# Fourier layer two: tile pairs in a written order of all engines, its second stage as seven block products, and third-sweep combinations kept by Fourier layer one

## The chip, the cores and the metric

The kernel runs on one core of one Trainium2 chip. The metric is the device time of one execution in microseconds; the time before is the median of three runs. The core has a matrix engine (PE, with its weight loads shown apart as PEld), a vector engine (DVE), an activation engine (ACT), GpSimd (POOL), and SyncE (SP), whose only work here is to issue DMA transfers. All data is float32; the matrix work is done in a split form, in which each operand is a rounded high part and a remainder, and three products (high·high, high·low, low·high) stand for one.

## The reference

Four layers in a row act on x (2048 rows of 640), each as `x = x + layer(layernorm(x))`: a sliding, dilated attention (A), a Fourier layer (B), and both again. The change is about the Fourier layers only:

```python
def _B_ref(x, dft_seq_re, dft_seq_im, dft_hid_re, dft_hid_im):
    a = jnp.einsum("bsd,ed->bse", x, dft_hid_re)
    b = jnp.einsum("bsd,ed->bse", x, dft_hid_im)
    y = jnp.einsum("ts,bse->bte", dft_seq_re, a) - jnp.einsum("ts,bse->bte", dft_seq_im, b)
    return y
...
x = x + _A_ref(_layernorm(x, axis=-1), A_wqkv, A_wo)
x = x + _B_ref(_layernorm(x, axis=-1), B_dft_seq_re, B_dft_seq_im, B_dft_hid_re, B_dft_hid_im)
x = x + _A_ref(_layernorm(x, axis=-1), A_wqkv, A_wo)
x = x + _B_ref(_layernorm(x, axis=-1), B_dft_seq_re, B_dft_seq_im, B_dft_hid_re, B_dft_hid_im)
```

## The kernel before

**Tiles.** The output of a Fourier layer is made in eight tiles of 256 rows, numbered 0 to 7. Each has two stages. The first multiplies the sequence matrices (real and imaginary, side by side as 512 columns) with the normalised x, and leaves five chunks of 128 hidden columns, called z, in PSUM. The second multiplies z with the hidden matrices and gives y: `ymm` takes a block of 128 rows, and for each of 5 chunks, 2 halves of 320 output columns, 3 split passes, and real and imaginary part issues one matmul 320 wide, so 60 for a block and 120 for a tile. `yout` adds y to x (a DVE addition for each half) and stores it.

**Pairs.** Tiles 0 and 1 are made on their own in `run`. Tiles 2 to 7 are made in three pairs by `pair`, and within a pair the first stage of chunks 0 to 3 is done as seven products of blocks instead of eight (m1 to m7, after Strassen's scheme). A pair has three sweeps, each over 8 steps i. In the first, products m5, m4 and m7 take 18 matmuls of width 512 a step; in the second, m2, m1 and the fifth chunk take 21; in the third, m3, m6 and the fifth chunk take 15. For each step, raw blocks of the sequence matrices are loaded (`s_raw`, the tile names are `win` and `xa`, seven buffers in all), partly combined by DVE (`combine`, line 1363), and split by ACT (the high part, line 1327) and DVE (the remainder, line 1328) into one of six views, two in tiles s0 and s1 and four in cells of the tiles r1_2 and r1_3. Combined blocks of x, which are made once in `run` and kept in HBM (`xc`), come back through `x_slot`. Behind each sweep, DVE and ACT put the products together from PSUM (lines 1421 to 1480) while PE does `ymm` of another block. In the third sweep, the first `ymm` of the pair's first tile is spread over the steps.

**Order.** Only PE's order is written out in a pair. The order of DVE, ACT and SP is chosen when the program is built, by a list scheduler with a timeline of its own. Each engine then executes its list strictly in order. In the attention layers the order of all engines is written out, step by step.

**Layers.** The class `LayerB` serves both Fourier layers: b1 (layer index 1) and b2 (layer index 3). The last pair of b1 is executed within the start of the second attention layer, which hangs its own first loads and transposes into it. The last tile of b2 has its second stage behind everything else, by `ytile` and `y_final`.

Of the kernel before, what the change touches and what calls it, by code (L numbers as in the profile page):

```python
# [20 lines left out]
D = 640  # L21
# [5 lines left out]
P = 128  # L27
# [130 lines left out]
    1: ((0, 0), (2, 1), 1),  # L158
    6: ((0, 1), (0, 0), -1),
}  # L160
NST = 16
FA = 64
GW = (512, 512, 512, 384)
# [6 lines left out]
def tile_layers(ctx: ExitStack, tc: tile.TileContext, x, wqkv, wo, cs, cst, wre, wim, out):  # L170
# [48 lines left out]
    xcb = [{m: dr.tile([P, NP, 2, 256], F32, name=f"xc_{l}_{m}") for m in XC} for l in range(2)]  # L219
# [846 lines left out]
    class LayerB:  # L1066
        def __init__(self, li):
            self.li = li
            self.xin, self.xout = xs[li], xs[li + 1]
            self.xn = {}  # L1070
            self.z = {}
            self.zt = {}
            self.xl, self.raw, self.ct = {}, {}, {}
            self.xc = xcb[li // 2]
            self.whole = {}
            self.ahead = {}
            self.late = []
            self.nraw = self.nhl = self.nx = self.nc_ = 0

        def ln_load(self, c, j):  # L1080
# [193 lines left out]
        def y_final(self, t):  # L1274
# [3 lines left out]
            for e in range(2):  # L1278
                o = xr[:, e * 320 : (e + 1) * 320]
                nc.vector.tensor_tensor(o, self.ym[e][:, :320], o, op=ALU.add)  # L1280
                nc.sync.dma_start(self.xout[c][:, j, e * 320 : (e + 1) * 320], o)

        def x_whole(self, side, i):
# [58 lines left out]
        def pair(self, p, nstats, hooks=None):  # L1342
# [53 lines left out]
            def ahead_b(i):  # L1396
# [3 lines left out]
                p22 = split(b22)  # L1400
                return x2, x1, p11, p22, lambda: (split(combine(b22, b11, b22, ALU.add)), split(b21))

            def ahead_c(i):
                b12, b22, b11 = raw(t2, i), raw(t2, NP + i), raw(t1, i)
                x6 = self.x_slot(6, i, ring)
                c3 = split(combine(b22, b12, b22, ALU.subtract))
                return x6, c3, split(b12), lambda: split(combine(b11, b11, b12, ALU.add))

            with tc.manual_schedule(engines={nc.tensor.engine}):
                m5, m4, m7 = banks("m0", "m1"), banks("xt", "t0"), banks("t1", "pq")  # L1410
                for i in range(NP):
                    ends = i == 0, i == NP - 1
                    x5, x7, c5, c4, c7 = self.ahead.pop(("a", p)) if i == 0 and ("a", p) in self.ahead else ahead_a(i)
                    self.product(m5, x5, c5, *ends)
                    self.product(m4, self.x_plain(*k2(i), 256), c4, *ends)
                    self.product(m7, x7, c7, *ends)
                    self.tick()
                b0 = ahead_b(0) if AH[0] else None
                m5s, m4s, ds = store("stg", CFG["bufs"]["stg"]), store("s2"), store("s3")
# [12 lines left out]
                for i in range(NP):  # L1432
# [5 lines left out]
                    c1, p21 = rest()  # L1438
                    self.product(m1, x1, c1, *ends)
                    self.product(f1, self.x_plain(*k2(i), 512), p21, False, i == NP - 1)  # L1440
                    self.tick()
                if hooks is not None:
                    views = cells[0] + cells[1] + CFG["views"]
# [50 lines left out]
        def run(self, nstats):  # L1494
# [6 lines left out]
            with ExitStack() as st:  # L1501
# [3 lines left out]
                for s in range(NST):  # L1505
# [6 lines left out]
                    self.z_mm(s, None, 1)  # L1512
                    self.tick()
                    for h in range(2):
                        ks = [k for k in range(KD) if R["y"][h][k] == s]
# [12 lines left out]
                self.evac(1)  # L1528
            for p in range(NPAIR - (nstats is not None)):
                self.pair(p, nstats)  # L1530

# [72 lines left out]
```

## Time and profile before

| what | value |
|---|---|
| median of three runs | 1736.29 us (1735.03, 1736.29, 1740.18) |
| span of the profiled execution, first to last instruction | 1734.8 us |
| PE busy | 1715.3 us of it |
| DVE, ACT, POOL busy | 1355.3, 824.7, 616.4 us |
| mean rate of the DMA engines | 242 GB/s |
| mean granted PE clock | 1.000 |
| b1's three pairs | from 455.6 us on, until about 855 us |
| b2's three pairs and its last tile | from 1313.1 us to the end |

The profile lists the busy time of each engine, then, for each line and shape of instruction, the count, the mean duration and what the engine waited for. Its windows give the same for any stretch of the span. The profiled execution's own time isn't listed apart; the median of the runs is 1.5 us above its span.

### The profile page before, as it was taken

The page shows a single profiled execution, that of the slowest core. Times are in us where ns is not written, and L with a number is a line of the kernel's source. Part 1 is how long each engine was busy: PE and PEld are TensorE (multiplying, and loading weights), DVE is VectorE, ACT ScalarE, POOL GpSimd, SP SyncE. Part 2 cuts the span into 40 slices and gives each one's busy share as a digit, 9 for nine tenths or more (in the row PEclk, how much of TensorE's full clock was granted, in tenths as well). Part 3 has the DMA queues.
Part 4 walks back from the last instruction along what each step waited for, and adds up shares of the span by engine and source line. Part 5 has one row for each costly group of instructions (what it writes and reads, how often), then busy time and mean ns, then how long its engine had stood idle before and what let it go on. Part 6 is the DMA issues. An engine that isn't in the chain of part 4 may idle for free.

```text
span 1734.8 us, 26552 instructions
## 1 busy us (share of the span) xinstructions
PE 1715.3 (99%) x8825; PEld 1496.1 (86%) x8825; DVE 1355.3 (78%) x2118; ACT 824.7 (48%) x1815; POOL 616.4 (36%) x570
## 2 busy tenths in 40 slices
PE   9999999999999999999999999999999999999999
PEld 7888888878888888888888889888888888888888
DVE  5999999978768667668639998899787677686673
ACT  5655645655445444445534434555444443443441
POOL 3899999940000000000019997899200000000000
PEclk9999999999999999999999999999999999999999
DMA  7768678959787687687547856698597867767761
GB/s 248 259 226 260 215 241 307 335 192 355 258 268 239 221 258 227 218 268 227 186 156 259 281 165 223 214 338 282 195 345 258 264 204 259 256 209 244 261 203 54
DMA packets 266713, 419.91 MB, mean 242 GB/s; under 512 B 22192, under 2 KB 144560, under 8 KB 266320
## 3 DMA queue, kind: packets, MB, share of 16 engines
q1 hardware_dynamic: 252400, 408.55, 71.2%
q10 hardware_dynamic: 14176, 9.67, 1.8%
q8 instruction: 70, 1.15, 0.3%
q14 instruction: 67, 0.55, 0.1%
HBM read 332.99 MB, written 85.14 MB: 241 GB/s over the span
## 4 chain that ended last, share of the span: by engine, by line
PE 86%; DVE 5%; POOL 3%; DMA 2%; issue 2%; ACT 2%; SPq 0%; DVEq 0%; ACTq 0%; POOLq 0%
PE m L499 18%; PE aux L1233 16%; PE t L1334 11%; PE m L1334 11%; PE aux L662 6%; PE pq L1334 6%; PE xt L1334 5%; PE m L1166 4%; PE t L1166 4%; PE xt L1166 2%; DVE pr L579 2%; DVE pr L622 1%; POOL pr L637 1%; POOL pr L582 1%; POOL pr L638 1%
## 5 line engine op out<-in xcount | busy, mean ns | idle before, releaser
L499 PE MATMUL m<-r,s 128*128 128x512 f32 (+1 forms) x1890 | 421.8, 378 | 0.2 <-ACT sg L514 0.2
L499 PEld LDWEIGHTS m<-r,s 128*128 128x128 f32 x1890 | 344.5, 188 | 54.7 <-ACT sg L514 1.6
L1327 ACT CAST r<-win 128x512 fp32r<-128x512 f32 x242 | 147.4, 621 | 168.2 <-DVE win L1363 80.4
L1233 PE MATMUL aux<-r2a,zo 128*128 128x320 f32 x768 | 226.0, 309 | 0.0
L579 DVE TENSOR_TENSOR pr<-pq,win 128x1280 f32<-128x1280 f32 x128 | 189.8, 1483 | 37.2 <-PE aux L1233 20.3
L637 POOL TENSOR_TENSOR pr<-pr 128x640 f32<-128x640 f32 x126 | 207.7, 1648 | 27.1 <-DVE pr L622 25.9
L1233 PE MATMUL aux<-pr,zo 128*128 128x320 f32 x704 | 208.0, 309 | 0.0
L582 POOL TENSOR_TENSOR pr<-pr 128x640 f32<-128x640 f32 x123 | 176.6, 1436 | 87.6 <-DVE pr L579 87.6
L622 DVE TENSOR_TENSOR pr<-pq,win 128x1280 f32<-128x1280 f32 x128 | 190.3, 1488 | 2.6
L1328 DVE TENSOR_TENSOR r<-win,r 128x512 fp32r<-128x512 f32 x242 | 162.7, 687 | 37.8 <-ACT r L1327 36.5
L300 POOL TENSOR_TENSOR stats<-stats,mhalf 128x1 f32<-128x1 f32 (+1 forms) x26 | 18.9, 728 | 445.9 <-ACT stats L294 445.9
L1334 PE MATMUL m<-r,r 128*128 128x512 f32 x600 | 153.0, 389 | 0.5 <-DVE r L1328 0.5
L1233 PEld LDWEIGHTS aux<-r2a,zo 128*128 128x128 f32 x768 | 144.1, 188 | 2.2
L1233 PEld LDWEIGHTS aux<-pr,zo 128*128 128x128 f32 x704 | 132.2, 188 | 2.4
L1334 PEld LDWEIGHTS m<-r,r 128*128 128x128 f32 x600 | 112.4, 188 | 24.0 <-DVE r L1328 1.0
L1334 PE MATMUL t<-r,r 128*128 128x512 f32 x492 | 132.0, 390 | 0.0
L638 POOL TENSOR_TENSOR pr<-pr 128x320 f32<-128x320 f32 x126 | 113.0, 897 | 9.9
L592 DVE TENSOR_REDUCE lg<-pr 128x64 f32<-128x640 f32 (+1 forms) x128 | 107.2, 837 | 11.4 <-POOL pr L582 11.3
L1363 DVE TENSOR_TENSOR win<-win,win 128x512 f32<-128x512 f32 x109 | 74.9, 691 | 49.9 <-DMA win<-cs_in 48.4
L1334 PEld LDWEIGHTS t<-r,r 128*128 128x128 f32 x492 | 92.4, 188 | 19.8
L1166 PE MATMUL m<-s,r 128*128 128x512 f32 x348 | 106.8, 395 | 1.7 <-ACT r L1103 0.9
L1166 PE MATMUL t<-s,r 128*128 128x512 f32 x348 | 105.2, 390 | 0.0
(299 smaller groups left out, 3245.6 us busy)
## 6 DMA issues: line engine op xcount, KB each, us to landing
win<-cs_in SPq DMA_DIRECT2D x346, 256.0 KB
r<-xc SPq DMA_DIRECT2D x240, 256.0 KB
win<-kvb SPq DMA_DIRECT2D x96, 440.0 KB
xa<-cs_in SPq DMA_DIRECT2D x120, 256.0 KB
win<-kvb SPq DMA_DIRECT2D x64, 360.0 KB
xc<-sg SPq DMA_DIRECT2D x28, 512.0 KB
xr<-xs SPq DMA_DIRECT2D x40, 320.0 KB
kvb<-stg SPq DMA_DIRECT2D x33, 320.0 KB
```

The lines of the kernel that those rows point to most:

```text
L499: nc.tensor.matmul(mt[g][:, : GW[q]], st[:, a, k], wq[q][:, b, k], start=n == 0, stop=n == 14)
L579: nc.vector.tensor_tensor(pr, q, wview(u, jp, 0, [[1, FE]]), op=ALU.mult)
L582: nc.gpsimd.tensor_tensor(pv[:, :, 0:10], pv[:, :, 0:10], pv[:, :, 10:20], op=ALU.add)
L592: nc.vector.tensor_reduce(rows(lgs[u], jp), pv.rearrange("p (a h) d -> p a h d", h=HE), axis=AX.X, op=ALU.add,)
L622: nc.vector.tensor_tensor(pr.rearrange("p j w (h d) -> p (j w) h d", d=DH), rows(lgs[u], jp).unsqueeze(3).to_broadcast([P, 2 * W, HE, DH]) ...
L637: g.tensor_tensor(pr[:, :, 0:4], pr[:, :, 0:4], pr[:, :, 4:8], op=ALU.add)
L638: g.tensor_tensor(pr[:, :, 0:2], pr[:, :, 0:2], pr[:, :, 2:4], op=ALU.add)
L1166: self.last = nc.tensor.matmul(self.z[t][k], self.xn[c][:, a, j, k * P : (k + 1) * P], self.ct[s][:, b], start=s == 0 and i == 0, stop=s = ...
L1233: self.last = nc.tensor.matmul(self.ym[e][:, :320], zt[(k, a, ri)][:, j2 * P : (j2 + 1) * P], w[:, e * 320 : (e + 1) * 320], start=(k, a, ...
L1327: nc.scalar.copy(hi, raw)
L1328: nc.vector.tensor_tensor(lo, raw, hi.bitcast(F32), op=ALU.subtract)
L1334: nc.tensor.matmul(bank, w(a, kb), hl[b], start=start and (a, b) == (0, 0), stop=stop and (a, b) == (1, 0),)
```

## The change

The pairs of b2, and its last tile, get a function of their own, `pairs7`. Fourier layer one keeps the old `pair`, with two additions. There are five parts.

1. **Order.** In `pairs7` the order of PE, DVE, ACT and SP is the order in which the code is written. Loads of a step are issued two steps ahead (`load(n + 2)`, `loadx(n + 2)`), and splits wait in a list (`fifo`) from which `fill` takes as many as there are free views, up to six.
2. **Second stage.** Of a tile's five chunks, the first three (`KS`) go through seven products of blocks: z is cut into 128-row halves and real and imaginary parts, the hidden matrices into halves of 320 columns. For each product 3 chunks × 3 passes are 9 matmuls; chunks 3 and 4 stay plain, with 12 matmuls for each of the four output blocks. The eight entries of `STAGES` name the bank's chain, the product, the plain block and the output block that is added afterwards. A chain goes on adding to the same bank after DVE has read it: chain 3 has four entries, chains 0 and 2 one, chain 1 two. Chains 0, 1 and 2 take bank aux0, chain 3 bank aux1.
3. **New operands.** `v_make` in b1 forms four combinations of the hidden matrices for each of the three chunks, splits them and stores them (`wvb`); `v_get` brings them back in the first pair of `pairs7`. `v_evac` replaces `zt_put`: it splits z as before, and forms and splits four sums for each of the three chunks.
4. **Kept combinations.** In the third sweep of b1's pairs, both combined sequence blocks of each step are stored to HBM (`keep`, `ccb`), and `pairs7` loads them instead of raw blocks, so that its third sweep has no `combine`. That lets the combined x of product m3, which was read plain from columns 0 to 255, come through `x_slot` as well (`x_keep`), and frees these columns for the operands of part 3.
5. **m6 into m1.** The product m6 goes on adding to m1's bank in place of a bank of its own.

```diff
+KS = (0, 1, 2)
+STAGES = (
+    (3, ("a11", "r0"), None, (0, 0)),
+    (0, ("a12", "i0"), (0, 0), (0, 0)),
+    (3, ("s2", "t2"), None, (0, 1)),
+    (1, ("s1", "t1"), None, (1, 1)),
+    (1, ("s4", "i1"), (0, 1), (0, 1)),
+    (3, ("s3", "u"), None, (1, 0)),
+    (2, ("a22", "t4"), (1, 0), (1, 0)),
+    (3, None, (1, 1), (1, 1)),
+)
...
+        def v_evac(self, t, raws, f, last=False):
...
+            def sums(raw, hi, lo, dg, ks):
...
+                v.tensor_tensor(a22, a21, a22, op=ALU.add)
+                v.tensor_tensor(a21, a21, a11, op=ALU.subtract)
+                v.tensor_tensor(a11, a11, a22, op=ALU.subtract)
+                v.tensor_tensor(a12, a12, a11, op=ALU.add)
...
+        def v_stage(self, t, n, tags=("aux0",) * 3 + ("aux1",)):
+            chain, prod, plain, (j, e) = STAGES[n]
...
+            if prod:
+                for k in KS:
+                    for a, b in PASSES:
+                        mms.append((self.zv[t][(prod[0], k)][a], self.wv[(prod[1], k)][b]))
...
+            h = self.half[(j, e)]
+            nc.vector.tensor_tensor(h, bank[:, :320], h, op=ALU.add)
...
+            def fill(most=99):
+                while fifo and held[0] < len(views) and most:
+                    fifo.pop(0)()
+                    held[0] += 1
+                    most -= 1
...
+                    product(bk["m3"], x[0], h("c3"), *ends)
+                    used()
+                    fill()
+                    product(bk["f2"], self.x_plain(*k1(i), 512), h("p12"), False, i == NP - 1)
+                    used()
+                    fill()
+                    product(bk["m1"], x[1], h("c6"), False, i == NP - 1, True)
+                    used()
+                    if 3 <= i < 6:
+                        self.v_stage(t1, (1, 0, 6)[i - 3])
+                    if i < NP - 1:
+                        continue
...
+                    for k, st in enumerate((2, 3, 5, 4, 7)):
+                        self.v_stage(t1, st)
...
+            def keep(i, n, raw):
+                nc.sync.dma_start(ccb[:, p, i, n], raw.rearrange("p r t -> p (r t)"))
...
+                    if i % 2 == 0 and 8 * p + i // 2 < 4 * len(KS):
+                        self.v_make(8 * p + i // 2)
...
+            if self.seven:
+                with tc.manual_schedule(engines=ENGINES - {nc.gpsimd.engine}):
+                    self.pairs7()
+                return
...
-    b2.ytile(NT - 1, 0, None)
-    b2.y_final(NT - 1)
```

What stands in the lists of the engines shows it at three places. The first is PE's list at the end of the third sweep of b2's first pair, before the change; t1 and m0, m1 are first-stage banks, aux0 and aux1 the second stage's.

```order
L1334 MATMUL t1_1949_13661<-r1_2_1732_12039,r1_1_1697_11760 128x512 x3
L1334 MATMUL m0_1995_14072<-r1_2_1732_12039,r1_1_1697_11760 128x512 x3
L1334 MATMUL m1_1996_14073<-r1_2_1732_12039,r1_1_1697_11760 128x512 x3
L1233 MATMUL aux0_2013_14198<-r2a_1821_12670,ot_1992_14056 128x320
L1233 MATMUL aux1_2014_14199<-r2a_1821_12670,ot_1992_14056 128x320
L1233 MATMUL aux0_2033_14397<-r2a_1821_12670,zo0_1989_14053 128x320
L1233 MATMUL aux1_2034_14398<-r2a_1821_12670,zo0_1989_14053 128x320
```

After the last 512-wide products come the last part of one `ymm` and then a whole `ymm` of 60 matmuls in new tiles of the two banks (one row stands for each run of matmuls). The same place of PE's list after the change:

```order
L1574 MATMUL t1_1981_13835<-r1_2_1750_12162,r1_1_1715_11883 128x512 x3
L1574 MATMUL m0_1977_13831<-r1_2_1750_12162,r1_1_1715_11883 128x512 x3
L1574 MATMUL m1_1978_13832<-r1_2_1750_12162,r1_1_1715_11883 128x512 x3
L1452 MATMUL aux1_2048_14436<-r1_0_1608_11228,zo0_2020_14227 128x320 x2
L1452 MATMUL aux0_2064_14598<-r2a_1839_12793,zo0_2020_14227 128x320 x2
L1452 MATMUL aux1_2048_14436<-r1_0_1608_11228,zo0_2020_14227 128x320 x2
L1452 MATMUL aux0_2064_14598<-pr0_1841_12798,zo0_2020_14227 128x320 x2
```

Entries 2, 3, 5 and 4 of `STAGES` follow, 9, 9, 9 and 21 matmuls, in turn on aux1 and aux0: the third goes on in the bank (buffer 2048) that the first filled, the fourth in that of the second. The second place is DVE's list there, first before the change (xt, t0, m0, m1 are the banks of m3 and m6, xr the rows of y).

```order
L1328 TENSOR_TENSOR r1_2_1732_12039<-xa_2029_14345,r1_2_1732_12039 128x2x256
L1477 TENSOR_TENSOR stg_1985_13977<-xt_1993_14070,stg_1985_13977 128x512
L1478 TENSOR_TENSOR s3_1941_13581<-xt_1993_14070,stg_1939_13579 128x512
L1480 TENSOR_TENSOR stg_1985_13977<-m0_1995_14072,stg_1985_13977 128x512
L1480 TENSOR_TENSOR stg_1985_13977<-m1_1996_14073,stg_1985_13977 128x512
L1246 TENSOR_TENSOR xr_2031_14384<-aux0_2013_14198,xr_2031_14384 128x320
```

A split into r1_2 stands ahead of the six instructions that put the products together, of which four are shown. DVE's list at this place after the change:

```order
L1520 TENSOR_TENSOR s1_2062_14565<-win_2060_14547,s1_2062_14565 128x512
L1515 TENSOR_TENSOR win_2060_14547<-win_2060_14547,win_2058_14543 128x512
L1520 TENSOR_TENSOR r1_2_1750_12162<-win_2059_14545,r1_2_1750_12162 128x2x256
L1515 TENSOR_TENSOR stg_2014_14149<-xt_2029_14243,stg_2014_14149 128x512
L1515 TENSOR_TENSOR s3_1969_13743<-t0_2030_14244,stg_1967_13741 128x512
L1515 TENSOR_TENSOR stg_2014_14149<-m1_1978_13832,stg_2014_14149 128x512
L1456 TENSOR_TENSOR xr_2018_14225<-aux1_2048_14436,xr_2018_14225 128x320
L1456 TENSOR_TENSOR qs_2019_14226<-aux0_2064_14598,qs_2019_14226 128x320
```

Three instructions that prepare the next sweep (the split into view s1, a combine, the split into r1_2) now stand directly ahead of those six, of which three are shown, and the addition that reads aux1 behind these. The third place is SP's list in the third sweep of b1's first pair, after the change (`cs_in` raw blocks, `xc` combined x).

```order
L1776 DMA win_878_5827<-cs_in 128x512
L1766 DMA r1_1_544_3397<-xc_0_6_123 128x2x256
L1863 DMA ccb_131<-win_875_5796 128x512
L1776 DMA xa_879_5829<-cs_in 128x512
L1863 DMA ccb_131<-xa_876_5798 128x512
L1776 DMA win_880_5831<-cs_in 128x512
```

The stores to `ccb` are new, two for each step, and stand between the loads.

More of the change, by code (lines that the diff above doesn't have):

```diff
@@ L218, in tile_layers @@
     qb = [[dr.tile([P, 2, NJ, FE], F32, name=f"qb_{c}_{q}") for q in range(NQ)] for c in range(NC)]
-    xcb = [{m: dr.tile([P, NP, 2, 256], F32, name=f"xc_{l}_{m}") for m in XC} for l in range(2)]
+    xcb = [{m: dr.tile([P, NP, 2, 256], F32, name=f"xc_{l}_{m}") for m in list(XC) + [3] * l} for l in range(2)]
+    wvb = dr.tile([P, len(KS), 4, 2, 320], F32, name="wvb")
+    ccb = dr.tile([P, NPAIR, NP, 2, 512], F32, name="ccb")
     c0b = dr.tile([P, NST, 2, 512], F32, name="c0b")
@@ L1405, in ahead_c, with rest @@
                 x6 = self.x_slot(6, i, ring)
-                c3 = split(combine(b22, b12, b22, ALU.subtract))
-                return x6, c3, split(b12), lambda: split(combine(b11, b11, b12, ALU.add))
+                keep(i, 0, combine(b22, b12, b22, ALU.subtract))
+                c3 = split(b22)
+                def rest():
+                    keep(i, 1, combine(b11, b11, b12, ALU.add))
+                    return split(b11)
+                return x6, c3, split(b12), rest
             with tc.manual_schedule(engines={nc.tensor.engine}):
@@ L1440, in pair @@
                     self.product(f1, self.x_plain(*k2(i), 512), p21, False, i == NP - 1)
+                    if i % 2 == 0 and 8 * p + 4 + i // 2 < 4 * len(KS):
+                        self.v_make(8 * p + 4 + i // 2)
                     self.tick()
@@ L1512, in run @@
                     self.z_mm(s, None, 1)
+                    if self.seven and 4 <= s < 4 + NP:
+                        self.x_keep(s - 4)
                     self.tick()
```

374 lines of the change are left out of this document (added).

## The prediction

> **What bounds the kernel now.** I read the page first, then the windows of the pairs, then the timeline at two places.
>
> ```profile
> span 1734.8 us, 26552 instructions
> PE 1715.3 (99%) x8825; PEld 1496.1 (86%) x8825; DVE 1355.3 (78%) x2118; ACT 824.7 (48%) x1815; POOL 616.4 (36%) x570
> PE 86%; DVE 5%; POOL 3%; DMA 2%; issue 2%; ACT 2%; SPq 0%; DVEq 0%; ACTq 0%; POOLq 0%
> ```
>
> PE is busy for all but 19.5 us, and the chain that ended last runs 86% over it. The windows below show that nearly none of the idle time lies in the pairs (columns: window, length, busy time of PE, PEld, DVE, ACT and POOL, granted clock, DMA share, GB/s). The first four rows are the three sweeps of b2's first pair and the `ymm` block behind the third; the last four are the sweeps of b1's first pair and the block ahead of its third sweep.
>
> ```profile
> 1313.10:1345.74 32.64, 32.42 (x143) 26.16 (x142) 23.29 (x38) 13.43 (x24) 0.00 (x0) 1.00 0.84 271
> 1354.54:1392.64 38.10, 38.10 (x172) 31.68 (x172) 25.13 (x39) 17.53 (x30) 0.00 (x0) 1.00 0.76 243
> 1401.44:1437.44 36.00, 36.00 (x181) 31.21 (x181) 24.74 (x43) 12.69 (x22) 0.00 (x0) 1.00 0.64 209
> 1437.44:1446.24 8.80, 8.80 (x58) 8.54 (x57) 7.79 (x14) 4.54 (x9) 0.00 (x0) 1.00 0.65 213
> 455.60:488.24 32.64, 32.57 (x145) 26.66 (x144) 23.85 (x39) 15.87 (x30) 0.00 (x0) 1.00 0.87 274
> 497.04:535.14 38.10, 38.10 (x171) 31.61 (x171) 26.44 (x42) 20.51 (x37) 0.00 (x0) 1.00 0.81 258
> 535.14:543.94 8.80, 8.80 (x61) 8.72 (x60) 8.80 (x16) 4.04 (x8) 0.00 (x0) 1.00 0.66 212
> 543.94:579.94 36.00, 36.00 (x181) 31.20 (x181) 23.30 (x40) 14.66 (x27) 2.10 (x2) 1.00 0.60 195
> ```
>
> So in the pairs a matmul removed is time won, as long as nothing that PE waits for comes later; and the reserve of the others is not large: DVE is busy for 0.71 of b2's first sweep, DMA for 0.84. Dividing rate by share, a full DMA moves about 325 GB/s (195/0.60; 271/0.84 is 323).
>
> What does a matmul cost when they follow each other?
>
> ```profile
> 1679.78 0.84 PE L1334 MATMUL t<-r,r 128*128 128x512 f32 x3
> ...
> 1681.14 1.52 PE L1334 MATMUL m<-s,r 128*128 128x512 f32 x6
> 1682.50 0.30 PE L1233 MATMUL aux<-r2a,zo 128*128 128x320 f32 x1
> ...
> 1684.11 0.31 PE L1233 MATMUL aux<-pr,zo 128*128 128x320 f32 x1
> 1684.26 0.85 PE L1334 MATMUL xt<-r,r 128*128 128x512 f32 x3
> ```
>
> Twelve of width 512 take 1682.50 - 1679.78 = 2.72 us, 0.227 each; twelve of width 320 take 1684.26 - 1682.50 = 1.76 us, 0.147 each. The durations (0.31) overlap and are not the price.
>
> **What the change removes.** For each of b2's tiles 2 to 7 the second stage falls from 120 matmuls of width 320 to 7 × 9 + 4 × 12 = 111. PE's list agrees: 1920 such matmuls in both Fourier layers before, 1200 + 666 now, 54 fewer. The first stage keeps its number (18 + 21 + 15 for a step). So 54 × 0.147 = **7.9 us** less on the path. The Trainium skill, page "TensorE: Matmul & The Clock Gate", section "Back-to-back issue gap", gives N/2.4 + 2.5 ns for an isolated matmul, 135.8 ns at 320 columns; by that the saving would be an estimated 7.3 us. The same section's sustained 131 ns at 512 columns isn't what this trace has (227 ns), so the row decides.
>
> **What it adds on DVE and ACT.** The third sweep loses two combines a step, 48 in all. Each tile gains the sums and their splits. For durations and spacing on DVE, I use the end of the third sweep in the first pair of b2:
>
> ```profile
> 1428.49 0.69 DVE L1328 TENSOR_TENSOR r<-xa,r 128x512 fp32r<-128x512 f32 x1
> 1434.12 0.69 DVE L1477 TENSOR_TENSOR stg<-xt,stg 128x512 f32<-128x512 f32 x1 [4.94 <-PE xt L1334]
> 1434.73 0.68 DVE L1478 TENSOR_TENSOR s<-xt,stg 128x512 f32<-128x512 f32 x1
> ...
> 1436.52 1.28 DVE L1480 TENSOR_TENSOR stg<-m,stg 128x512 f32<-128x512 f32 x2
> 1437.72 0.49 DVE L1246 TENSOR_TENSOR xr<-aux,xr 128x320 f32<-128x320 f32 x1
> L1212 DVE TENSOR_TENSOR zo<-s,zo 128x256 fp32r<-128x256 f32 x15 | 6.0, 419 | 1.1 <-PE aux L1233 0.6 <-ACT zo L1207 0.5
> 1435.97 0.62 ACT L1327 CAST r<-win 128x512 fp32r<-128x512 f32 x1
> ```
>
> A DVE instruction over 512 lasts 0.69 us and they follow each other at 0.61; 256 last 0.42; an addition of 320 lasts 0.49; a split by ACT 0.62. From 256 and 512, at 0.27 for each further 256, 1024 would last some 1.2 and 128 some 0.28. `v_evac` then costs a tile about 8 us of DVE (one of 1024, four of 512, six of 256, five of 128), where five splits of 512 cost 3.5 before. A pair therefore gains 9 us there and 4 in eight more additions, and loses 16 × 0.69 = 11: even. The sums of tile t2 fall into the next first sweep, whose DVE work is 8 × 5 × 0.61 = 24.4 plus 8, within 32.6 of products and 3.1 of entry 1. I cost this at nothing; what hides it is the two steps of splits that lie ready.
>
> **The waits it adds.** Before, a whole `ymm` of 60 matmuls, 8.8 us, stood behind each sweep in banks of its own; whatever DVE did meanwhile cost nothing. Now entries 2, 3, 5, 4, 7 stand there, and entry 5 adds to the bank that entry 2's addition must first have read. Between them PE has 18 matmuls, 2.64 us. On DVE, that addition is queued behind all that the list puts ahead of it. Take T as the end of the third sweep's last product (nine matmuls, 2.04 us, after m3's last). The view s1 is free at T - 1.9 (with 0.16 for the matmul's own tail). Then ACT's copy to -1.2; DVE's split, combine and split start at -1.16, -0.55 and +0.06; the six that put the products together at 0.66 and every 0.60 on until 3.67; the addition runs from 4.27 to 4.76. Before, the six could start at m3's end, as the idle 4.94 us ahead of the first shows. PE reaches entry 5 at T + 2.64 and stands until about 4.85: **2.2 us**, in pairs one and two, so 4.4. The third pair has no next sweep to prepare; its six start at T - 1.85 and the addition ends at 2.0, in time. Bounds: 0, if DVE gets its splits earlier than I think, and 4 for each, if the raw blocks for that combine land late.
>
> Behind the second sweep of pairs two and three, the same link: the last split starts at T - 0.4, four instructions follow, the addition ends at T + 3.1, PE stands for some 0.5 us: 1.0 in all (0 to 2). Behind the first sweep, only entries 0 and 6 follow, in different banks, and the next products' banks are free at T + 2: nothing. The last tile runs its eight entries over four banks; entry 0 wants aux1, which the addition of the previous tile's entry 7 frees at T + 12.0, PE is there at 11.9: 0.2 (0 to 2). Behind the last addition, one store ends the program as before.
>
> **The DMAs it adds.** One transfer costs SP's queue 0.33 to 0.38 us to issue, five a step are 1.9 us of 3.4: no bound.
>
> ```profile
> L1317 SPq DMA_DIRECT2D win<-cs_in x312: 327/332/1278, 428.0 to 1686.6; - x156
> L1307 SPq DMA_DIRECT2D r<-xc x240: 370/383/1347, 396.8 to 1686.1; - x120
> ```
>
> Bytes are closer. In b1, `v_make` moves 1.97 MB for a chunk (two loads and four stores of 0.328), 60 GB/s over a first sweep: 274 + 60 = 334 of 325, so about 0.9 us too much, and as much again in the second pair's first sweep. `keep` adds 4.2 MB to each third sweep, 116 GB/s: 195 + 116 = 311, just under. I put **2 us** on b1 (0 to 13, below). In b2's first pair the third sweep has five transfers of 0.262 MB and two of 0.164 a step, 13.1 MB or 40 us at 325 GB/s, against 34.7 of sweep and 8.8 of entries: 1 us (0 to 3) where it runs late.
>
> **Sum.** The span lacks 1.5 us to the median of the runs, which I carry unchanged: 1736.3 - 7.9 + 4.4 + 1.0 + 0.2 + 2 + 1 = **1737.0**.
>
> **Rivals.**
>
> *The waits are hidden.* If the additions reach their banks in time, and DMA keeps up, some 1 us is lost: 1736.3 - 7.9 + 1 = 1729.4. For it: DVE is idle for a quarter of these sweeps. Against it: DVE's written order, in which the addition can't pass what stands ahead.
>
> *b1's third sweeps become bound by DMA; slower.* In steps 0 to 2 there is no `ymm` between, so a step lasts 15 × 0.227 = 3.4 us; four loads and now two stores of 0.262 MB take 1.57/325 = 4.84 us. That is 1.44 × 3 steps × 3 pairs = 13 us in place of my 2: 1748. It decides if the loads lead by less than one step when the sweep begins: a store must leave a raw buffer before it can be loaded again, and there are seven. Half of it gives 1742.5. Against it: a whole `ymm` block ahead of the sweep, in which the DMA share was 0.66.
>
> *PE's clock.* A stop of PE of 2 us or more could cost clock afterwards. If the clock halves for as long as PE stood, 15 matmuls cost 0.147 more in each pair, 4.4 us with both: 1741.4. The row against it is the start of the kernel, where PE is busy for 3.69 us of 5 and the clock stays at 1.00:
>
> ```profile
> 0.00:5.00 5.00, 3.69 (x12) 1.45 (x13) 1.66 (x8) 1.73 (x4) 1.34 (x11) 1.00 0.64 196
> ```
>
> The Trainium skill's page "TensorE: Matmul & The Clock Gate", section "What's actually happening", has the clock halved after an idle window of about 3.4 us; by that rule stops of 2.2 us would cost nothing, stops of twice that might.
>
> *The new operands are slow.* t2, t4 and u lie in pieces of 80 columns. If such a matmul cost as much as one of 512, 27 × 6 × 0.08 = 13 us would be added: 1750. Against it: operands in pieces of 256 (r views) and whole ones (s views) take the same 389 ns today.
>
> ```profile
> L1334 PE MATMUL m<-r,r x600: 388/389/499, 455.6 to 1697.8; 128*128 128x512 f32 x150
> L1334 PE MATMUL m<-s,r x264: 389/389/398, 509.7 to 1703.0; 128*128 128x512 f32 x132
> ```
>
> **Chances.** A measurement of this kernel can tell about 0.3%, 5.2 us, from no change: 1731.1 to 1741.5. Forecast 0.58 (its own range 1732 to 1742), hidden waits 0.21, DMA in b1 0.12, clock 0.06, slow operands 0.03. Faster is the hidden waits, 0.21; slower is DMA and operands, half of the clock's case, which ends at the edge, and none of the forecast, 0.18; same is the rest, 0.61. The range takes half of the case of hidden waits below and half of the slower ones above: 1730 to 1745.
>
> **What would show it.** The saving: 666 matmuls of line 1452 at 0.147 apart. The waits: PE idle before line 1452, released by DVE's additions (line 1456), 2 us at a time, twice behind a third sweep. b1: PE idle in the windows of its pairs, with the DMA share at 0.9 and more. I am wrong if PE's idle time before line 1452 is below 2 us in all, or if idle time appears in the first stage's products of `pairs7` (line 1574), waiting for DVE or ACT, which I put at 1 us.

## The result and the profile after

The changed kernel is **slower**: 1750.57 us (median of four runs, 1748.35 to 1751.07) against 1736.0 of the kernel before (four runs, 1735.03 to 1740.18), a ratio of 1.0075 with a 95% interval of 1.0061 to 1.0089. The forecast was 1737.0 and the range ended at 1745. The profiled execution took 1748.35 us, its span 1746.6.

The page of the profile after, the lines that answer to those of before:

```profile
span 1746.6 us, 26782 instructions
PE 1712.0 (98%) x8771; PEld 1489.9 (85%) x8771; DVE 1370.6 (78%) x2166; ACT 834.9 (48%) x1838; POOL 614.7 (35%) x570
PE 72%; DMA 10%; DVE 10%; issue 3%; ACT 3%; POOL 2%; SPq 1%; ACTq 0%; DVEq 0%; POOLq 0%
```

54 matmuls fewer, as the change says. But PE's idle time rose from 19.5 to 34.6 us, and the chain that ended last, which ran 86% over PE, now runs 72% over it, with 10% each over DMA and DVE. The windows say in which stage. The columns are those of before; the first four rows are the first, second and third sweep of b2's first pair and the entries behind the third; the last three are b1's first pair: second sweep, the `ymm` block ahead of the third sweep, third sweep.

```profile
1315.95:1349.57 33.62, 32.95 (x146) 26.97 (x145) 26.49 (x42) 14.96 (x26) 0.00 (x0) 1.00 0.86 285
1358.37:1396.47 38.10, 38.10 (x170) 31.55 (x169) 26.30 (x39) 19.81 (x33) 0.00 (x0) 1.00 0.98 323
1405.27:1443.64 38.37, 35.32 (x173) 29.84 (x172) 21.59 (x40) 15.29 (x27) 0.00 (x0) 1.00 0.99 322
1443.64:1462.04 18.40, 11.48 (x62) 10.73 (x60) 11.27 (x19) 3.91 (x7) 0.00 (x0) 0.81 0.53 191
495.92:534.02 38.10, 37.80 (x168) 31.06 (x167) 27.78 (x49) 20.79 (x42) 0.00 (x0) 1.00 0.93 318
534.02:543.80 9.78, 9.78 (x66) 9.56 (x65) 9.78 (x18) 5.12 (x10) 0.00 (x0) 1.00 1.00 345
543.80:579.80 36.00, 36.00 (x182) 31.21 (x181) 25.03 (x44) 14.53 (x27) 1.74 (x2) 1.00 0.87 298
```

In b2's first pair the second and third sweep run with the DMA engines full (0.98 and 0.99). The third sweep stands for 3 of its 38.37 us. The entries behind it take 18.40 us, 6.9 of them idle, and PE's granted clock is 0.81 on their average. In b1 the DMA share is up from 0.81, 0.66 and 0.60 to 0.93, 1.00 and 0.87, and PE hardly stands. The list of PE's waits (what waited, for what; us in all, times, the longest) has these ahead of everything that both kernels share:

```profile
PE aux L1452 <- DVE xr L1456: 6.4, 4, 3.7
PE aux L1452 <- DMA r2a<-wvb: 3.2, 1, 3.2
PE xt L1574 <- DMA r<-xc: 3.1, 2, 1.6
```

And PE's timeline behind the third sweep, first in pair one, then in pair two (start, length, instruction, count, in brackets the idle time ahead of it and what ended it):

```profile
1449.20 1.00 PE L1452 MATMUL aux<-r2a,zo 128*128 128x320 f32 x3 [3.21 <-DMA r2a<-wvb]
1453.88 2.23 PE L1452 MATMUL aux<-r,zo 128*128 128x320 f32 x7 [3.67 <-DVE xr L1456]
...
1456.44 2.24 PE L1452 MATMUL aux<-pr,zo 128*128 128x320 f32 x9
1458.52 0.31 PE L1452 MATMUL aux<-r2a,sg 128*128 128x320 f32 x1
...
1589.39 1.29 PE L1452 MATMUL aux<-r,zo 128*128 128x320 f32 x7 [2.23 <-DVE xr L1456]
```

Pair two has the wait that I forecast, 2.23 us, and nothing else of note. Pair one has it at 3.67, behind a wait of 3.21 for t1 that I didn't forecast, and then matmuls that follow each other more slowly: the 18 from 1453.88 to 1458.52 take 4.64 us, where at 0.147 each they would take 2.65. From the start of b2's pairs to the end, the trace has 1746.6 - 1315.95 = 430.65 us against 1734.8 - 1313.11 = 421.69 before: 8.96 more, in spite of 7.9 saved, so some 17 us of new waits. 13.2 of them lie in pair one's third sweep and its entries (38.37 + 18.40, against 34.76 + 8.79 in experiment e6 below, where they run without a wait). The rest of the span's difference, 2.8 us, has arisen by the time b2's pairs begin.

The late t1 and r<-xc lead to SP. Its list around the second stage behind b2's second sweep (SPq: when each DMA was issued and how long the issue took), first before, then after:

```profile
1391.33 0.38 SPq L1307 DMA_DIRECT2D r<-xc  x1
1393.58 0.33 SPq L1317 DMA_DIRECT2D win<-cs_in  x1
1394.00 0.39 SPq L1307 DMA_DIRECT2D r<-xc  x1
1395.96 0.93 SPq L1317 DMA_DIRECT2D xa<-cs_in  x2
1400.76 0.93 SPq L1317 DMA_DIRECT2D win<-cs_in  x2
1405.99 0.34 SPq L1253 DMA_DIRECT2D y_out<-xr  x1
```

```profile
1392.90 0.87 SPq L1352 DMA_DIRECT2D r<-wvb  x2
1393.82 0.47 SPq L334 DMA_DIRECT2D xr<-xs  x1
1405.99 0.35 SPq L1268 DMA_DIRECT2D y_out<-xr  x1
1406.44 1.10 SPq L1494 DMA_DIRECT2D win<-ccb  x1
...
1444.28 0.81 SPq L1354 DMA_DIRECT2D r2a<-wvb  x2
```

In both, the store of y can't be issued before 1405.99, when DVE's addition behind `ymm` is done. Before, the list scheduler had put loads for the coming sweep ahead of it. Now the order of the code is SP's order, and the loads for the coming steps stand behind the store: SP issues nothing for 11.7 us, and from 1393.6 to 1406.0 the DMA engines have a share of only 0.29. The last row shows a second thing: t1's six loads stand last among the 24 loads of the second stage's operands, and the last two of them are issued at 1444.28, when the third sweep's products are over (1443.64). That gave a theory with three parts for pair one (the store in SP's list; the 24 loads of the second stage's operands inside sweeps that are full already; the splits ahead of the put-together operations on DVE), and a fourth, apart from them, for what the change adds ahead of b2's pairs. The rival: the pair's bytes are simply too many, wherever they are issued.

### The profile page after: what moved, and what is told of

The parts are those of the page before. It is cut to its first block, busy times and chain, and to the rows that moved or that the text cites. A ratio compares the mean times of both kernels' runs of the same rounds, so it can differ in the third digit from the quotient of the medians.

```text
span 1746.6 us, 26782 instructions
## 1 busy us (share of the span) xinstructions
PE 1712.0 (98%) x8771; PEld 1489.9 (85%) x8771; DVE 1370.6 (78%) x2166; ACT 834.9 (48%) x1838; POOL 614.7 (35%) x570
## 3 DMA queue, kind: packets, MB, share of 16 engines
q8 instruction: 70, 1.15, 0.3%
## 4 chain that ended last, share of the span: by engine, by line
PE 72%; DMA 10%; DVE 10%; issue 3%; ACT 3%; POOL 2%; SPq 1%; ACTq 0%; DVEq 0%; POOLq 0%
PE m L512 19%; PE aux L1248 7%; PE aux L675 6%; PE t L1574 5%; PE m L1574 5%; PE aux L1452 4%; PE m L1793 3%; DMA win<-cs_in 3%; PE t L1793 3%; PE m L1181 3%; PE pq L1574 3%; PE t L1181 3%; PE xt L1574 2%; PE xt L1793 2%; PE xt L1181 1%
## 5 line engine op out<-in xcount | busy, mean ns | idle before, releaser
L1248 PE MATMUL aux<-r2a,zo 128*128 128x320 f32 x480 | 141.4, 309 | 0.0
L1248 PE MATMUL aux<-pr,zo 128*128 128x320 f32 x440 | 130.1, 309 | 0.0
L526 ACT COPY stg<-m 128x480 f32<-128x480 f32 x96 | 53.5, 557 | 94.0 <-PE m L512 88.2
L1248 PEld LDWEIGHTS aux<-r2a,zo 128*128 128x128 f32 x480 | 90.1, 188 | 1.4
L1248 PEld LDWEIGHTS aux<-pr,zo 128*128 128x128 f32 x440 | 82.6, 188 | 1.6
L675 PE MATMUL aux<-r2a,ot 128*128 128x320 f32 x540 | 83.7, 310 | 0.0
L675 PEld LDWEIGHTS aux<-r2a,ot 128*128 128x128 f32 x540 | 80.4, 188 | 1.5 <-ACT wa L498 0.3
```

The source lines that it names most:

```text
L675: nc.tensor.matmul(m[:, :320], oT[(c, j)][:, a, k], wo_s["w"][:, b, k, e * 320 : (e + 1) * 320], start=(i, k) == (0, 0), stop=(i, k) == (2 ...
L1248: self.last = nc.tensor.matmul(self.ym[e][:, :320], zt[(k, a, ri)][:, j2 * P : (j2 + 1) * P], w[:, e * 320 : (e + 1) * 320], start=(k, a, ...
```

## The experiments

The twelve were timed in three groups, e1 to e4, e5 to e8 and e9 to e12, each on a chip of its own beside the kernel before. us is the median; the medians of before lie between 1735.9 and 1736.6. By the intervals, the difference of two runs is known to some 3 to 4 us.

| run | us | ratio to before, 95% interval |
|---|---|---|
| the change | 1750.6 | 1.0075, 1.0061 to 1.0089 |
| e1 loads between | 1758.2 | 1.0127, 1.0113 to 1.0142 |
| e2 no early splits | 1745.2 | 1.0047, 1.0031 to 1.0064 |
| e3 both | 1751.8 | 1.0087, 1.0073 to 1.0101 |
| e5 stores deferred | 1745.5 | 1.0046, 1.0033 to 1.0060 |
| e12 = e2 + e5 | 1738.6 | 1.0013, 1.0003 to 1.0024 |
| e6 = e12 + loads between | 1734.0 | 0.9982, 0.9970 to 0.9993 |
| e11 = e6, x stores later | 1736.3 | 0.9991, 0.9981 to 1.0002 |
| e10 = e6 without kept sums | 1761.4 | 1.0143, 1.0130 to 1.0157 |
| e4 b1's and run's part only | 1743.8 | 1.0041, 1.0028 to 1.0055 |
| e7 of it, keeping only | 1739.8 | 1.0016, 1.0006 to 1.0026 |
| e8 of it, making only | 1738.0 | 1.0005, 0.9996 to 1.0013 |
| e9 of it, x stores only | 1737.5 | 1.0008, 0.9999 to 1.0016 |

### e1: the loads between the sweeps, and e3: with e2

In `pairs7` the loads of t4, t2 and u leave the sweeps:

```diff
-                if p == 0 and sw > 0:
-                    for _ in range((0, 1, 2)[sw]):
-                        if gets:
-                            self.v_get(*gets.pop(0))
+                if p == 0 and sw == 2 and gets:
+                    self.v_get(*gets.pop(0))
...
                         self.yout(tp, 0, None)
+                        for _ in range(9):
+                            self.v_get(*gets.pop(0))
...
                         self.yout(tp, 1, None)
                         self.v_halves()
+                        for _ in range(9):
+                            self.v_get(*gets.pop(0))
```

> The 18 loads of t4, t2 and u are issued in the two stretches between the sweeps of b2's first pair (nine in each, while the second stage of tile 1 runs, DMA share 0.34 and 0.31 in after) and t1's six one a step from the third sweep's first step on; nothing else is changed. Theory A (these loads, in sweeps whose DMA share is 1.0 already, are what costs the first pair its 10 us: two waits for r<-xc, 1.57 and 1.48, one for t1, 3.21, a late chain on DVE, 3.67, and slow matmuls behind the stop, some 2.6): all goes but a wait of about 2.2 for DVE, so some 8 to 10 us less than after: 1741 to 1743, the PE idle time that r<-xc and r2a<-wvb release below 1 us in the first pair. Rival B (the bytes of the pair are too many wherever they are issued): the wait moves to the start of the next sweep, 0 to 3 us less than after: 1748 to 1751.

Measured: 1758.2, slower than the change by 7.6, against both theories. SP's list in e1, around the same place:

```profile
1399.57 1.25 SPq L1768 DMA_DIRECT2D r<-xc  x2
1400.87 0.46 SPq L334 DMA_DIRECT2D xr<-xs  x1
1414.53 0.35 SPq L1268 DMA_DIRECT2D y_out<-xr  x1
1414.93 1.66 SPq L1354 DMA_DIRECT2D r<-wvb  x3
...
1420.05 0.50 SPq L1354 DMA_DIRECT2D qs<-wvb  x1
1420.65 0.37 SPq L1494 DMA_DIRECT2D win<-ccb  x1
```

My edit had put the nine loads behind `yout`, so behind its store. They were issued from 1414.93 on, when the third sweep had already begun, and that sweep's own loads had to wait until they were out: PE stood 7.10 us for r<-xc there, and 3.81 us in the second sweep, ahead of which my edit had put the other nine. The run didn't test the bytes; what it shows is that a place in SP's list ahead of or behind a waiting store matters more than the stage in which the load stands.

> The two edits together. Theory A: the loads are worth 8 to 10 us and the splits another 2 to 4 (2.2 in each of pairs one and two): 1737 to 1740, equal to the kernel before within 0.3%; what is left against 1728.4 (before less 7.9) is some 5 us in b1 and in b2's run and some 3 of small waits. If both rivals held: 1748 or more.

Measured: 1751.8, for the same reason 12 us above what the theory had. Against e1 the late splits gain 6.5.

### e2: no splits ahead of the put-together operations

```diff
-                fill()
+                if sw < 2 or i < NP - 1:
+                    fill()
...
                     product(bk["m3"], x[0], h("c3"), *ends)
                     used()
-                    fill()
+                    if i < NP - 1:
+                        fill()
```

and the same behind the product with p12.

> In the last step of each third sweep of b2's pairs one and two no further splits for the next sweep are put ahead of the six operations that put the products together; they follow in the second stage's entries. Nothing else is changed. Theory A (PE stands before entry 5 since DVE's addition of entry 2 is queued behind splits and six put-together operations): pair two's 2.23 us before line 1452 go to below 0.5; of pair one's 3.67 some 2 go; total 1746 to 1748. Rival B (the splits that are put off are missing at the start of the next first sweep): the same 2 us appear before the first products of the next pair, 1750 or more. Rival C (DVE isn't the cause, the wait stays): 1750.

Measured: 1745.2, 5.4 less than the change, where theory A had 1746 to 1748. DVE's and PE's timelines in pair two:

```profile
1580.74 0.68 DVE L1520 TENSOR_TENSOR s<-win,s 128x512 fp32r<-128x512 f32 x1
1581.34 0.68 DVE L1515 TENSOR_TENSOR stg<-xt,stg 128x512 f32<-128x512 f32 x1
...
1583.73 1.28 DVE L1515 TENSOR_TENSOR stg<-m,stg 128x512 f32<-128x512 f32 x2
1585.34 0.49 DVE L1456 TENSOR_TENSOR xr<-aux,xr 128x320 f32<-128x320 f32 x1 [0.33 <-PE aux L1452]
```

```profile
1585.14 1.48 PE L1452 MATMUL aux<-r2a,zo 128*128 128x320 f32 x9
1586.46 1.19 PE L1452 MATMUL aux<-r,zo 128*128 128x320 f32 x7
```

The six operations start as soon as m3's bank is done, the addition of entry 2 now waits for PE (0.33) and not the reverse, and entry 5 follows entry 3 without a stop. The wait didn't come back at the next sweep. So the place of the splits in DVE's list was the cause, as the prediction had it.

### e5: the two stores of tile 1 two steps later

```diff
-                        self.yout(tp, 0, None)
+                        self.yout(tp, 0, None, 2)
...
-                        self.yout(tp, 1, None)
+                        self.yout(tp, 1, None, 2)
...
                 self.v_flush()
+                self.tick()
```

> After, with only the two stores of tile 1 in b2's first pair (y_out<-xr behind the first and the second sweep) issued two steps later, at the next sweep's second step. Theory A (SP issues in a written order now; each of these stores waits some 13 us for DVE's addition, and the loads of x, of the raw blocks and of the second stage's operands that stand behind it are late: in e1 SP stood from 1401.3 to 1414.5 and r<-xc came 7.1 us late): the two waits of after for r<-xc (1.57 and 1.48) go, and with an earlier queue part of the 3.21 for t1 and of DVE's lateness: 3 to 8 us less than after, 1743 to 1747. Rival B (the DMA engines are full in the third sweep, share 1.0, and set its pace whatever the queue's order): within 1.5 us of after, 1749 to 1751.

Measured: 1745.5, 5.1 less than the change. The waits for r<-xc are gone, and the one for t1 is down from 3.21 to 1.57, though the third sweep's DMA share is still 0.92. In the 12.5 us ahead of that sweep the share is 0.91, where the change has 0.35. Theory A holds; the DVE wait stays (3.72), which is e2's matter.

### e12 and e6: all of it, with the loads in the sweeps or between them

e12 is e2 and e5 together. e6 has e1's loads as well, but ahead of the second stage's load of x, which the store follows:

```diff
+                        for _ in range(9):
+                            self.v_get(*gets.pop(0))
                         self.ymm(tp, 0, 0, KD)
...
+                        for _ in range(9):
+                            self.v_get(*gets.pop(0))
                         self.ymm(tp, 1, 0, KD)
```

> After, with the stores deferred, the late splits of e2, and the 18 loads of t4, t2 and u issued ahead of the second stage's load of x in each of the two stretches (nine and nine, ahead of what waits there), t1's six one a step from the third sweep's first step on. Theory A: the first pair loses neither r<-xc nor t1 (below 1 us of PE idle time in the third sweep and its entries together), and what is left over the kernel before is b1's part, some 8 us by e4, against 7.9 saved: 1735 to 1738. Rival B (bytes): 1743 or more, r<-xc or r2a<-wvb still late by 3 us and more.

> e6 with the 24 loads of the second stage's operands where after has them (one and two a step in the second and third sweep), so only the stores' place in SP's list and the late splits are mended. e2 alone is worth 5.4 us and e5 alone 5.1. Theory A (the stores were the trouble in the queue; the loads then fit): 1734 to 1737, within 2 us of e6. Rival B (their bytes in sweeps with a DMA share of 1.0 cost by themselves): 1738 to 1742, r2a<-wvb late by 1.5 us or more, as in e5.

Measured: e12 1738.6, e6 1734.0 (one of its twelve executions took 7498 us, for which I have no reading; the median of the other eleven is 1733.4, and the differences below use that). In e12, whose profiled execution was its longest (1743.32), the wait for t1 is 2.84 us still; in e6 there is none. The windows of e6's third sweep of pair one and of its entries:

```profile
1405.93:1440.69 34.76, 34.76 (x173) 29.98 (x172) 25.70 (x46) 16.90 (x30) 0.00 (x0) 1.00 0.98 336
1440.69:1449.48 8.79, 8.79 (x62) 8.79 (x60) 4.95 (x10) 0.85 (x2) 0.00 (x0) 1.00 0.36 111
```

Both are PE's bare work. So the bytes of the whole pair fit, and the rival is out. With the loads where the change has them the time is 1738.6 - 1733.4 = 5.2 us longer. From the start of b2's pairs to the end e6 takes 1731.5 - 1316.62 = 414.9 us, 6.8 less than before, of 7.9 that the matmuls save; e12 takes 1741.4 - 1321.19 = 420.2. What in the loads costs these 5 us isn't told apart, since e6 moves the 18 loads out of the sweeps and also issues t1's six earlier. In e12 the last two of these six are issued at 1445.56, as late as in the change; in e6 the last one is issued some 12 us before the third sweep ends:

```profile
1428.49 0.42 SPq L1354 DMA_DIRECT2D r2a<-wvb  x1
```

A run with only t1's loads moved ahead would tell. The edits from the change to e6 gain 17.2 us: 5.4 and 5.1 by e2 and e5 alone, 5.2 by the loads, and the remainder, 1.5, isn't told apart. What keeps e6 from being 7.9 us faster than before is mainly what the change adds ahead of b2's pairs (e4 below).

### e10: without the kept combinations

b2's third sweep loads raw blocks and combines two of them a step, as before; b1 keeps nothing.

```diff
-                    raws[n] = [pre(p, i, 0), self.s_raw(t2, i, wide), pre(p, i, 1)]
+                    raws[n] = [self.s_raw(*a, wide) for a in ((t2, NP + i), (t2, i), (t1, i))]
...
+                def d0():
+                    b22, b12, b11 = raws[n]
+                    combine(b22, b12, b22, ALU.subtract)
+                    half(n, "c3", b22)
```

> e6 without the kept combinations: b1 stores none, and b2's third sweep loads three raw blocks a step and combines two of them on DVE, as the kernel before did. Theory A (the keeping stores cost 3.2 us in b1 and DVE has the time for the combines in b2, 77% busy): 1730 to 1732, 2 to 4 less than e6. Rival B (DVE is bound there: 16 more instructions of 0.61 us spacing in a sweep, 9.8 us, ahead of the same additions, so PE waits for them): 1738 to 1745, idle time before the first stage's products and before line 1452 in b2's third sweeps.

Measured: 1761.4, 28 us more than e6: rival B, and far beyond its price. DVE's timeline in the third sweep of pair one:

```profile
1418.86 0.69 DVE L1515 TENSOR_TENSOR win<-win,win 128x512 f32<-128x512 f32 x1
1420.37 0.69 DVE L1520 TENSOR_TENSOR s<-win,s 128x512 fp32r<-128x512 f32 x1 [0.82 <-ACT s L1519]
...
1422.69 0.68 DVE L1515 TENSOR_TENSOR win<-xa,win 128x512 f32<-128x512 f32 x1
1424.19 0.69 DVE L1520 TENSOR_TENSOR s<-win,s 128x512 fp32r<-128x512 f32 x1 [0.82 <-ACT s L1519]
```

In the written order a combined block goes DVE (combine), ACT (high part), DVE (remainder) with nothing between, so DVE stands 0.82 us for ACT each time: some 2.1 us for a combined block from the combine's start to the next instruction, not two times 0.61. Two such blocks are 4.2 us, and a step's products take PE 3.4. From the start of b2's pairs to the end e10 takes 447.0 us, 32 more than e6. PE's waits explain some 18 of it: 11.9 before line 1452, in stops of up to 3.1 us, and 6.8 before the third sweeps' products, against 0.5 and nothing in e6. The other 13.5 are busy time of PE, 423.9 us against 410.4 for the same 2084 matmuls, with the granted clock at 0.50 behind the four longest stops.

### e4, e7, e8, e9: what the change adds ahead of b2's pairs

e4 keeps b1's stores and the making of the operands and the eight stores of x, and gives b2 the pairs and the last tile of before, which read none of it. e7, e8 and e9 have one of the three each.

```diff
-            if self.seven:
-                with tc.manual_schedule(engines=ENGINES - {nc.gpsimd.engine}):
-                    self.pairs7()
-                return
```

> All that the change adds ahead of b2's pairs (the keeping stores of b1's third sweeps, the making of t4, t2, u and t1, the eight stores of x in b2's run) stays, and b2's pairs and last tile are as in the kernel before, which don't read what was kept. Theory A (these transfers cost b1's pairs 2.5 us and b2's run 2.4 us on PE, as after's trace has it against before's): 1736 + 4 to 6 = 1740 to 1742. Rival B (the difference of the two traces there is jitter from one execution to the next): 1736 to 1737. My prediction had put 2 us on it: 1738.

> As e4 (b2's pairs as in the kernel before), but of the three additions only the keeping stores of b1's third sweeps (48 of 0.262 MB). Theory A (all three cost in proportion to their bytes, 12.6, 5.9 and 2.1 MB, of e4's 7.9 us): 4.8 us, 1740 to 1742. Rival B (only the making of the operands costs, since it puts DVE and ACT work and stores into sweeps that are short of DMA time already, 334 of 325 GB/s by my prediction): 1736 to 1737. Rival C (the stores hold the raw buffers, my prediction's case of a step bound by DMA): 1743 and more, nearly all of e4.

> As e4, but of the three additions only the making of t4, t2, u and t1 in b1's first two pairs (twelve operands, 5.9 MB). Theory A (bytes): 2.3 us, 1738 to 1739. Rival B (the making costs all): 1743. Rival C (the keeping stores cost all): 1736.

> As e4 (b2's pairs as in the kernel before), but of the three additions only the eight stores of x in b2's run (2.1 MB, steps 4 to 11). e4 cost 7.9 us, the keeping stores alone 3.2, the making alone 1.4. Theory A (the costs add up): 3.3 us, 1739 to 1740, on c0b's late blocks in the run. Rival B (they don't add: keeping and making hurt more together, since they meet in the first two pairs of b1): 1736 to 1737.

Measured: e4 7.9 us over before by the medians (by the ratio's interval 4.9 to 9.5), e7 3.2, e8 1.4, e9 1.2, which sum to 5.8; the intervals of e8 and e9 both reach just below 1. That is three to four times what I had put there, with the most for the keeping stores, which move the most bytes. e7 and e8 rule out that the stores or the making cost nearly all, and e9's theory A (3.3) lies outside its interval. Whether the three hurt more together than alone is within the intervals; and since the profiled execution of e4 is its fastest (1739.66), its trace holds only 3 us of the difference. e7's profiled execution is near its median (1740.63), and its span is 4.0 above that of before. In b1's pairs and the start of the attention behind them, PE has four waits of more than 0.5 us there, 1.63, 0.81, 1.15 and 1.44, where before has two, 0.54 and 0.92: 3.6 more. The longest lies in the third sweep of b1's first pair, behind a combine of DVE that waited for its raw block:

```profile
556.89 0.69 DVE L1822 TENSOR_TENSOR win<-win,win 128x512 f32<-128x512 f32 x1 [2.78 <-DMA win<-cs_in]
558.24 1.45 PE L1793 MATMUL m<-r,r 128*128 128x512 f32 x5 [1.63 <-DVE r L1787]
```

So in e7, which differs from the kernel before by these stores alone, a raw block lands late; the stores stand between the loads in SP's list. This is one execution, so a difference between executions isn't excluded, and where e8 and e9 lose their part isn't shown.

### e11: the stores of x later in the run

```diff
-                    if self.seven and 4 <= s < 4 + NP:
-                        self.x_keep(s - 4)
+                    if self.seven and 8 <= s < 8 + NP:
+                        self.x_keep(s - 8)
```

> e6 with the eight stores of x in b2's run at steps 8 to 15 in place of 4 to 11. Theory A (in steps 4 to 11 they meet a DMA share of 0.96 and make c0b's blocks late, 1.3 us in e6): 1 to 2 us less than e6, 1732 to 1733. Rival B (the same bytes cost the same there, or meet the last tiles' loads): 1734 or more.

Measured: 1736.3, no gain on e6 (the intervals overlap). The wait for c0b in the list of waits is 0.7 us where e6 has 1.3, and the time didn't follow. Rival B.

**e6** is the fastest version: 0.18% faster than the kernel before (0.07 to 0.30%), and 17.2 us faster than the change.

## Why the prediction was wrong

- **The matmuls, -7.9.** Right: 54 fewer, and in e6, where nearly nothing waits, b2's pairs and last tile are 6.8 us shorter with some 1.2 us of named waits left (0.7 ahead of the first product, 0.5 before line 1452).
- **The wait behind the third sweep, 4.4 in two pairs.** The mechanism was right, and shown by e2. Pair two has 2.23 where the sum had 2.2. Pair one has 3.67: DVE's splits came later since their raw blocks did, the case that the prediction gave for its upper bound ("4 for each, if the raw blocks for that combine land late"). That the bound held is luck: the addition of entry 2 ends at 1453.82, 7.5 us after PE could have begun entry 5 (1443.64 + 2.64 = 1446.28), and only the wait for t1 ahead of it hides the rest. Both pairs' waits taken away are worth 5.4.
- **Behind the second sweep, 1.0, and the last tile, 0.2.** 0.25 and 0.24 us in pairs two and three by the list of waits (0.41 and 0.40 from start to start), half of the 0.5 each that was put. In the last tile no wait is listed.
- **DVE's load, "even", at nothing.** In the change's own order it cost nothing that shows. But the working missed what the kept combinations are worth: I counted 16 combines at 0.69, 11 us a pair of DVE time off the path; e10 shows 28 us on the path. That this is since the written order has no work between the halves of a combined split is argued from DVE's timeline, not tested apart.
- **b1's DMAs, 2 (0 to 13).** Mis-sized: 5.8 by the parts, 7.9 by e4. The rival's 13 us didn't come: in the change's trace PE is busy for all of 36.00 us in the first third sweep. But a late raw block, its mechanism, is there in small in e7's trace, with the stop of 1.63 us in the first third sweep.
- **The step that failed: b2's first pair, "1 us (0 to 3)".** The prediction set "13.1 MB or 40 us at 325 GB/s, against 34.7 of sweep and 8.8 of entries". Two things were wrong in it. It let the transfers use the time of the entries, but the last loads in the list are t1's, which entry 3 wants at the start of them, and x and the raw blocks are wanted inside the sweep. And it took SP's queue as free ("five a step are 1.9 us of 3.4: no bound"): it counted the time of issuing, not what stands ahead. With the store of y at the head for 11.7 us, the loads for the sweep were issued when it began, and the DMA engines, with a share of 0.29 from 1393.6 to 1406.0, were full behind it. In place of 1 us the runs show 5.1 for the stores (e5) and 5.2 for the loads (e12 to e6: their bytes in the sweeps and t1's late place together). In the change's trace pair one loses 13.2 us, where the sum had 2.2 + 1; with b1's 5.8 in place of 2, that is about the 13.6 us by which the time missed the forecast.
- **PE's clock, a rival at 0.06.** It happened, as a consequence of the longer stop: 2.0 us in pair one. It isn't the cause of the result.

One of the forecast's own signs pointed at the right place for the wrong reason: idle time before line 1574 was 3.8 us, where I had put 1, but I had named DVE or ACT as what would be waited for. Only 0.7 waited for DVE (ahead of the first product), and 3.1 for a DMA, r<-xc.

## What to carry to other kernels

When a change gives an engine a written order, read its list for instructions that wait, and ask what stands behind each: a store that waits for its result belongs behind the loads that the next stage needs. Compare bytes with time up to the moment when the last of them is wanted, not over the stage as a whole, and look which load stands last in the list. And move one thing at a time with the queue's list beside it: e1 had the right idea and lost 7.6 us by its place behind one store.

## What the hardware showed beyond that

The granted clock of PE can fall to half behind stops little longer than those of the forecast, but the length of a stop alone doesn't decide it. 2.23 us cost nothing in the change, nor did 2.77 in e1 (before 1462.88; the clock is 1.00 in all windows from 1462 to 1468). 2.84 cost clock in e12, and so did two stops of 2.39 in e10 (before 1539.54 and 1683.43; 0.50 from 1541 to 1543 and from 1685 to 1687). The windows (the seventh column after the window is the granted clock) behind pair one's and pair two's stop in the change:

```profile
1452.00:1454.00 2.00, 0.12 (x1) 0.13 (x1) 2.00 (x5) 0.54 (x1) 0.00 (x0) 0.50 0.31 106
1456.00:1458.00 2.00, 2.00 (x9) 2.00 (x8) 1.09 (x2) 0.00 (x0) 0.00 (x0) 0.50 0.00 0
1458.00:1460.00 2.00, 2.00 (x15) 2.00 (x15) 0.00 (x0) 0.00 (x0) 0.00 (x0) 0.97 0.23 82
1588.00:1590.00 2.00, 0.61 (x4) 0.61 (x5) 1.73 (x4) 0.62 (x1) 0.00 (x0) 1.00 0.38 132
1590.00:1592.00 2.00, 2.00 (x16) 2.00 (x15) 0.99 (x2) 0.00 (x0) 0.00 (x0) 1.00 0.03 8
```

After stops of 3.21 and 3.67 us with three matmuls between, the clock is 0.50 for some four microseconds of work, and 18 matmuls cost 2.0 us more; after 2.23 it stays at 1.00. In e12 a stop of 2.84 was enough (the matmuls behind it, and the window):

```profile
1450.46 1.13 PE L1452 MATMUL aux<-r2a,zo 128*128 128x320 f32 x3 [2.84 <-DMA r2a<-wvb]
```

```profile
1451.00:1453.00 2.00, 1.63 (x6) 1.24 (x7) 0.90 (x2) 0.00 (x0) 0.00 (x0) 0.55 0.16 58
```

In e1, behind a stop of 3.81 that ended at 1374.74, the clock fell only when PE had worked again for over a microsecond:

```profile
1374.00:1376.00 2.00, 1.26 (x6) 1.07 (x7) 1.29 (x2) 0.79 (x2) 0.00 (x0) 1.00 0.95 312
1376.00:1378.00 2.00, 2.00 (x7) 1.58 (x6) 0.87 (x2) 1.44 (x3) 0.00 (x0) 0.56 1.04 374
```

The Trainium skill, page "TensorE: Matmul & The Clock Gate", section "What's actually happening", has the clock watched in free-running windows of about 3.4 us and halved after an idle one; the delay in e1 fits windows that run free of the kernel, and such windows would also explain why 2.77 us left the clock alone where 2.39 us halved it; no run here tests this. But the stops of 2.39 and 2.84 us are shorter than the page's window and still cost the clock. The page's other figure, in "Why this matters for your kernels", no gaps above some 3 us, is nearer to what was measured here, though these two stops lie below it as well.
